# Seven row maxima in a visit: the idle token bank of an MLP's second phase used for one more score matmul

## The chip, the cores and the metric

The kernel runs on one core of a Trainium2 chip. The metric is the device time of one launch in microseconds (us), as the median of several runs. Engines go by the profile's names: PE is TensorE's matmuls, PEld its weight loads, DVE is VectorE, ACT ScalarE, POOL GpSimd and SP the queue that issues most DMAs. PSUM, into which TensorE writes, has 8 banks of 512 fp32 columns on 128 partitions. The kernel holds all of it as one tile, `bank[:, 0..7]`.

## The reference

For 2048 tokens of width 448, with x the common input:

```
g = sigmoid(sum(x * gate_w))
a = mha_block(x)                 # 16 heads of 28: qkv, softmax(q k^T * 28^-0.5), p v, wo
h = gelu(layernorm(x) @ w1 + b1) # 448 -> 1792, tanh form
b = h @ w2 + b2                  # 1792 -> 448
out = g * a + (1 - g) * b
```

The kernel's softmax subtracts the maximum of each query's row of scores. These maxima are the work that the change regroups: 16 heads x 16 query tiles of 128 x 4 pieces of 512 keys, so 1024 score matmuls of [28 x 128] by [28 x 512], each with a maximum over its 512 columns.

## The kernel before, in words

The work runs in three stages: projections of q, k, v; the MLP, during which nearly half of the row maxima are taken; and attention, during which the rest are taken. The core's instructions stand in program order on every engine from the third token chunk of the projections on, and on TensorE throughout.

**The MLP** works on four chunks c of 512 tokens, each in two phases. In the first (`mlp1`, line 564) each of 14 feature tiles f takes 11 matmuls of 512 columns into bank `f % 2`, from which ScalarE takes two gelus. In the second (`mlp2`, line 579) each of four token tiles i takes 14 x 3 = 42 matmuls of 448 columns (lines 585, 586 and 590) which accumulate in bank `i % 2`; ScalarE then copies that bank out (line 596). So in the second phase one of the banks 0 and 1 accumulates, and the other holds the last tile until it is copied and then nothing until the next tile begins.

**Row maxima beside the MLP.** After matmuls of the MLP the kernel calls `filler.run(n)` (line 449), which adds n to a slot counter. `due` (line 442) spreads the maxima evenly over the slots of the whole MLP: `MLP_MAX` = 482 of them over about 248 slots, where a matmul of the second phase counts 0.205 (line 590's call adds that, the call before it twice that). When as many are due as a visit takes (`MG` = 6, or what is left), a **visit** is issued: `RowMax.issue(2, 6)` (line 374) puts six score matmuls (line 402) into banks 2 to 7, between two matmuls of the MLP. The four heads of a group lie in four strips of 32 rows of the array; successive score matmuls go round them (head j in rows 32j to 32j+27). Every 65th place in this order holds instead a transpose of 16 finished columns (`close`, line 366).

**The maxima on VectorE.** `reduce` in `issue` takes the banks in order, two at a time where it can: line 384 reduces two neighbouring banks in one instruction, line 382 one bank. Two are taken together only if the second's place in `mx` lies after the first's, which fails each time the heads wrap from 3 to 0 between them. A score matmul waits for the reduce that read its bank in the visit before; `close` adds `mt` (line 371), and the last of 64 pieces adds `mf` (line 418).

**After the MLP** attention issues single maxima into banks 5 and 6 (`scores`, line 515) until all 1040 places are done. The first five scores of attention are put beside the last token tile (line 594). Bank 7 serves that tile and then the sums of p v.

The lines that set the order of the visits:

```
            if self.max is not None and self.due(n) >= min(MG, self.upto - self.done) > 0:
                self.max.issue(2, min(MG, self.upto - self.done))
...
        due = self.first + (self.upto - self.first) * min(1, self.slot / self.slots) - self.done
```

Of the kernel before, what the change touches and what calls it, by code (L numbers as in the profile page):

```python
# [26 lines left out]
NF = F // P  # L27
# [5 lines left out]
MG = 6  # L33
FS = 4
W1, W2 = 0.233, 0.205
# [6 lines left out]
def kernel(ctx: ExitStack, tc: tile.TileContext, xt, wqk, wv, wo, xk, w1, b1, w2, b2,  # L42
# [300 lines left out]
    class RowMax:  # L343
# [27 lines left out]
            nc.vector.tensor_scalar(mt, ps[:4 * TPC, :P], -1.0, None, op0=OP.mult)  # L371
            self.queue.dma_start(ms[g][:, c * CH:(c + 1) * CH].rearrange("j (i x) -> j i x", x=P), mt.bitcast(F32))

        def issue(self, first, n, rows=None):

            held = []

            def reduce():
                if held:
                    (b0, c0), (b1, c1) = held[0], held[-1]  # L380
                    if b0 == b1:
                        nc.vector.reduce_max(self.mx[:, c0:c0 + 1], bank[:, b0], axis=AX)  # L382
                    else:
                        nc.vector.reduce_max(self.mx[:, c0:c1 + 1:c1 - c0], bank[:, b0:b1 + 1], axis=AX)  # L384
                    held.clear()

            for b in range(first, first + n):
                if self.done >= NG * NC * 65:
                    break
                self.done += 1  # L390
                left = sum(len(x) for x in self.left)
                if self.last is not None and (left <= 56 or self.n == NG * NC):
                    reduce()
                    self.close(bank[:, b])
                    continue
                most = max(range(4), key=lambda j: (len(self.left[j]), -j))
                j = max(rows, key=lambda j: len(self.left[j])) if rows else most
                if not self.left[j]:
                    j = most
                i, k = self.left[j].pop(0)  # L400
                r = slice(32 * j, 32 * j + DH)
                nc.tensor.matmul(bank[:, b], self.qds[self.n][r, i * P:(i + 1) * P],  # L402
                                 khi[self.n // NC][r, k * 512:(k + 1) * 512], start=True, stop=True)
                at = (j * TPC + i) * 4 + k
                if held and held[0][1] > at:
                    reduce()
                held.append((b, at))
                if len(held) == 2:
                    reduce()
                if left == 41 and self.n + 1 < NG * NC:  # L410
                    self.load(self.n + 1)
                g, c = divmod(self.n, NC)
                if c == NC - 1 and g < MLP_G and all(n != k for x in self.left for _, n in x):
                    load_khr(g + 1, k)
                if left == 1:
                    reduce()
                    self.last = mpool.tile([P, 4 * TPC], F32, name="mf")
                    nc.vector.reduce_max(self.last, self.mx.rearrange("p (a k) -> p a k", k=4), axis=AX)
                    if self.n + 1 < NG * NC:
                        self.begin(self.n + 1)  # L420
                    else:
                        self.n += 1
                        self.left = [[]] * 4
            reduce()

    class Filler:
# [19 lines left out]
            left = self.upto - self.done  # L446
            return left if self.slot >= self.slots else min(left, int(due))

        def run(self, n=1):


            if self.max is not None and self.due(n) >= min(MG, self.upto - self.done) > 0:
                self.max.issue(2, min(MG, self.upto - self.done))

    filler = Filler()

# [3 lines left out]
    def load_khr(g, k=None, queue=nc.sync):  # L460

        sl = slice(0, S) if k is None else slice(k * CH, (k + 1) * CH)
        for j in range(4):
            r = D + (4 * g + j) * DH
            queue.dma_start(khr[32 * j:32 * j + DH, sl].bitcast(F32), qk[0, r:r + DH, sl])
# [38 lines left out]
    def load_qm(n):  # L504

        while filler.done < min(65 * NG * NC, 65 * (n + 1) + 9):
            filler.max.issue(5, 1)
        g, c = divmod(n, NC)
        nc.sync.dma_start(qs[n][0][DH:P:32].bitcast(F32), ms[g][:, c * CH:(c + 1) * CH])

# [4 lines left out]
    def scores(units, most, tiles, between=None):  # L515

        def product(p, i):
            u = units[p]  # L520
            n, k, j = u // 4 // NT, u // 4 % NT, u % 4
            g, (qh, ql) = n // NC, qs[n]
            a, b, r = ((khi[g], qh, DH + 1), (klo[g], qh, DH), (khi[g], ql, DH))[i]
            r = slice(32 * j, 32 * j + r)
            nc.tensor.matmul(bank[:, p], a[r, k * P:(k + 1) * P], b[r], start=(i == 0), stop=(i == 2))  # L525

        def exps(at):
            t = tiles(len(at), at[0])
            nc.scalar.activation(t, bank[:, at[0]:at[-1] + 1], AF.Exp, scale=SCALE)  # L529
            for i, p in enumerate(at):  # L530
                probs[units[p]] = t[:, i]

        first, last = list(range(len(units)))[:UA], list(range(len(units)))[UA:]
        if most > 0:
            filler.max.issue(5, 1, [(units[0] + 3) % 4])
        for i in range(3):
            for p in first:
                product(p, i)
        exps(first)
        if between:  # L540
            between()
        for i in range(3):
            for p in last:
                product(p, i)
            if i == 0 and most > 1:
                filler.max.issue(6, 1, [(units[0] + 1) % 4, (units[0] + 2) % 4])
        if last:
            exps(last)
        if most > 2:
            filler.max.issue(5, 1, [(units[0] + 1) % 4, (units[0] + 2) % 4])  # L550


    ml = ExitStack()
# [25 lines left out]
    def mlp2(c, i):  # L579

        sl = slice(i * P, (i + 1) * P)
        last = c * TPC + i == NT - 1
        a = bank[:, 7 if last else i % 2, :D]
        for f in range(NF):
            nc.tensor.matmul(a, hh[f][:, sl], w2h[f], start=(f == 0), stop=False)  # L585
            nc.tensor.matmul(a, hh[f][:, sl], w2l[f], start=False, stop=False)  # L586
            rows = not last and (c * TPC + i < NT - 2 or f < 10) and (c + i > 0 or f > 3)
            if rows:
                filler.run(2 * W2)
            nc.tensor.matmul(a, hl[f][:, sl], w2h[f], start=False, stop=(f == NF - 1))  # L590
            if rows:
                filler.run(W2)
            if last and f == NF // 3:
                scores(list(range(U)), 0, early)
        gb = mh.tile([P, CH], F32, name="h", bufs=2)[:, :D]
        nc.scalar.activation(gb, a, AF.Copy)  # L596
        nc.sync.dma_start(gbs[c * TPC + i], gb)

    with texts:
# [12 lines left out]
        for c in range(NC):  # L612
# [23 lines left out]
            if c == NC - 1:  # L636
                m0.close()
                aq = ctx.enter_context(tc.tile_pool(name="aq", bufs=1, side="right", reuse_waits="tile"))

                first = {3: aq.tile([P, S], F32, name="klo", bufs=2), 2: aq.tile([P, NT, P], F32, name="vg", bufs=2)}  # L640

                def early(n, p):
                    t = first[n] if n == 3 else first[n].rearrange("p a b -> p (a b)")
                    return t[:, :n * CH].rearrange("p (n c) -> p n c", c=CH)

                nc.scalar.activation(gate, zall, AF.Exp, scale=-1.0)
                load_khi(0)
                load_klo(0)
                load_q(0)
                load_v(0)  # L650
                load_qm(0)
            else:
                ln_load(c + 1)
                ln_fetch(c + 1, 0)
                ln_fetch(c + 1, 1)
            for i in range(TPC):
                mlp2(c, i)
                if c == NC - 1 and i == 0:
                    nc.vector.tensor_scalar_add(gate, gate, 1.0)
                    nc.vector.reciprocal(gate, gate)  # L660
                    nc.vector.tensor_scalar(ngate, gate, -1.0, 1.0, op0=OP.mult, op1=OP.add)
                if c + 1 < NC and i < 3:
                    ln_apply(c + 1, i)
                    if i < 2:
                        ln_fetch(c + 1, i + 2)
                    else:
                        ln_apply(c + 1, 3)
# [125 lines left out]
    with tc.manual_schedule(engines=ENGINES):  # L793
# [3 lines left out]
        at = -1  # L797
# [3 lines left out]
        while u < 4 * steps:  # L801
# [3 lines left out]
            units = list(range(u, min(u + (UL if late else U), 4 * steps)))  # L805
            while at < units[-1] // 4:
                at += 1
                n, k = divmod(at, NT)
# [43 lines left out]
            if u:  # L852
                scores(units, min(3, filler.due()), pt, (lambda: values(ready - 1)) if late else None)
# [3 lines left out]
            if ended:  # L857
                n = summed // NT - 1
# [62 lines left out]
```

## Time and profile before

| | |
|---|---|
| Median of 3 runs | 1119.53 us (1119.23 to 1121.82) |
| The profiled execution | 1119.32 us, of which the span of its instructions is 1117.5 us |
| PE busy | 1105.8 us (99%) |
| DVE, ACT, POOL busy | 738.9 us (66%), 634.4 us (57%), 333.4 us (30%) |
| Granted TensorE clock | 1.0 of full speed in all slices |
| The four second phases of the MLP | begin at 158, 247, 337 and 427 us of the span |

A timeline row gives the start in us from the beginning of the span, the length in us, the engine, the line of the kernel, the operation, the tile written <- the tiles read, shapes, and "xN" where neighbouring instructions of one kind are merged; in brackets stands how long the engine was idle before it, and what ended that. A row of a merged group has one start and the length until the last of the group ends. A matmul's length is modelled and holds its way through the array, so matmuls that follow each other overlap: their starts are what one reads. A row of the groups by line gives a count, the summed busy time, the mean of one in ns, and the idle time before them.

### The profile page before, as it was taken

How to read it: one execution, taken by the hardware profiler on the slowest of the kernel's cores; microseconds unless marked ns; L12 is line 12 of the kernel's file. 1: busy time of each engine (PE TensorE's matmuls, PEld its weight loads, DVE VectorE, ACT ScalarE, POOL GpSimd, SP SyncE). 2: the span in 40 equal slices, each digit the busy share in tenths (PEclk: the TensorE clock that was granted, in tenths of full speed). 3: DMA queues.
4: the chain of work that ended last, by engine and by line, in shares of the span. 5: the costliest groups of instructions: out<-in, count | busy, mean ns of one | idle time of the engine just before them, and what ended most of it. 6: DMA issues, size and time to landing. Idle time of an engine off the chain costs nothing.

```text
span 1117.5 us, 19782 instructions
## 1 busy us (share of the span) xinstructions
PE 1105.8 (99%) x8136; PEld 672.7 (60%) x8136; DVE 738.9 (66%) x1029; ACT 634.4 (57%) x662; POOL 333.4 (30%) x354
## 2 busy tenths in 40 slices
PE   7999999999999999999999999999999999999998
PEld 5888777777777777744444444444444444454546
DVE  3534398988889889576766766676667767746103
ACT  5324551230241132288787877887877878847572
POOL 4006665343334331013113221320223024342350
PEclk9999999999999999999999999999999999999999
DMA  8988541011120113163100220012021003002111
GB/s 263 302 273 309 170 135 58 9 47 36 50 55 32 30 43 96 38 157 89 28 18 19 61 69 22 22 28 52 26 60 36 18 20 94 12 26 70 55 32 58
DMA packets 53079, 84.35 MB, mean 75 GB/s; under 512 B 8516, under 2 KB 28500, under 8 KB 52076
## 3 DMA queue, kind: packets, MB, share of 16 engines
q1 hardware_dynamic: 48732, 76.27, 22.7%
q0 software_dynamic: 4256, 6.81, 2.5%
q8 instruction: 64, 1.05, 0.4%
q14 instruction: 27, 0.22, 0.1%
HBM read 56.40 MB, written 26.49 MB: 74 GB/s over the span
## 4 chain that ended last, share of the span: by engine, by line
PE 96%; DMA 2%; DVE 1%; ACT 1%; POOL 0%; SPq 0%; issue 0%
PE bank L788 22%; PE bank L525 20%; PE bank L402 16%; PE bank L572 13%; PE bank L207 5%; PE bank L590 5%; PE bank L585 4%; PE bank L586 4%; PE bank L223 3%; PE bank L693 1%; PE bank L694 1%; PE bank L695 1%; DMA raw<-in_xt 1%; DMA raw<-in_wqk 1%; DMA raw<-in_wv 0%; DMA s<-in_w 0%
## 5 line engine op out<-in xcount | busy, mean ns | idle before, releaser
L529 ACT ACTIVATE pt<-bank 128x1536 f32<-128x1536 f32 (+1 forms) x387 | 461.9, 1244 | 141.0 <-PE bank L525 140.8
L382 DVE TENSOR_REDUCE mx<-bank 128x1 f32<-128x512 f32 x618 | 409.6, 687 | 173.1 <-PE bank L402 159.1
L788 PE MATMUL bank<-pt,vg 128*32 128x512 f32 x1950 | 261.6, 602 | 0.0
L384 DVE TENSOR_REDUCE mx<-bank 128x2 f32<-128x1024 f32 x203 | 238.9, 1219 | 29.2 <-PE bank L402 28.8
L402 PE MATMUL bank<-khi,qd 28*128 28x512 f32 x512 | 241.7, 479 | 0.1
L402 PEld LDWEIGHTS bank<-khi,qd 28*128 28x128 f32 x512 | 92.3, 181 | 148.1 <-DVE mx L382 106.9
L525 PE MATMUL bank<-qh,klo 28*128 28x512 f32 x1024 | 174.7, 393 | 0.0
L525 PE MATMUL bank<-qh,khi 29*128 29x512 f32 x768 | 157.2, 480 | 0.0
L572 PE MATMUL bank<-y,w1f 128*128 128x512 f32 x616 | 152.4, 398 | 1.1 <-ACT h L576 1.1
L572 PEld LDWEIGHTS bank<-y,w1f 128*128 128x128 f32 x616 | 112.5, 188 | 34.8 <-issue 10.9
L525 PE MATMUL bank<-ql,khi 28*128 28x512 f32 x768 | 129.6, 390 | 0.0
L577 POOL TENSOR_TENSOR hl<-h,hh 128x512 fp32r<-128x512 f32 x56 | 73.7, 1317 | 117.5 <-ACT h L576 77.3
L788 PEld LDWEIGHTS bank<-pt,vg 128*32 128x32 f32 x1950 | 44.6, 108 | 77.2 <-issue 76.7
L525 PEld LDWEIGHTS bank<-qh,klo 28*128 28x128 f32 x1024 | 87.6, 185 | 4.0
L575 ACT ACTIVATE hh<-bank,b1s 128x512 fp32r<-128x512 f32 x56 | 38.5, 687 | 90.3 <-PE bank L572 90.3
L709 POOL DMA_DIRECT2D lt<-ob x15 | 10.9, 725 | 250.9 <-DVE ob L708 250.9
L596 ACT ACTIVATE h<-bank 128x448 f32<-128x448 f32 x16 | 8.7, 545 | 134.5 <-PE bank L590 100.2
L590 PE MATMUL bank<-w2h,hl 128*128 128x448 f32 x224 | 85.0, 379 | 0.0
L525 PEld LDWEIGHTS bank<-qh,khi 29*128 29x128 f32 x768 | 60.8, 181 | 39.6 <-ACT pt L529 26.7
L585 PE MATMUL bank<-w2h,hh 128*128 128x448 f32 x224 | 83.3, 372 | 0.0
L586 PE MATMUL bank<-w2l,hh 128*128 128x448 f32 x224 | 81.9, 365 | 0.0
L402 PE MATMUL bank<-khr,qd 28*128 28x512 f32 x512 | 80.1, 467 | 0.2 <-DVE mx L384 0.2
(122 smaller groups left out, 1294.6 us busy)
## 6 DMA issues: line engine op xcount, KB each, us to landing
qk<-hl SPq DMA_DIRECT2D x28, 512.0 KB
raw<-in_xt SPq DMA_DIRECT2D x16, 256.0 KB
vs<-vt SPq DMA_DIRECT2D x16, 256.0 KB
s<-in_xt SPq DMA_DIRECT2D x16, 256.0 KB
rc<-rls POOLq DMA_DIRECT2D x60, 64.0 KB, 2.2
bxr<-in_xk SPq DMA_DIRECT2D x8, 448.0 KB
gbs<-h SPq DMA_DIRECT2D x16, 224.0 KB
klo<-qk SPq DMA_DIRECT2D x16, 224.0 KB
```

The costliest lines, as they stand in the source:

```text
L207: nc.tensor.matmul(ps, a, b, start=(i == 0), stop=(i == len(ops) - 1))
L382: nc.vector.reduce_max(self.mx[:, c0:c0 + 1], bank[:, b0], axis=AX)
L384: nc.vector.reduce_max(self.mx[:, c0:c1 + 1:c1 - c0], bank[:, b0:b1 + 1], axis=AX)
L402: nc.tensor.matmul(bank[:, b], self.qds[self.n][r, i * P:(i + 1) * P], khi[self.n // NC][r, k * 512:(k + 1) * 512], start=True, stop=True)
L525: nc.tensor.matmul(bank[:, p], a[r, k * P:(k + 1) * P], b[r], start=(i == 0), stop=(i == 2))
L529: nc.scalar.activation(t, bank[:, at[0]:at[-1] + 1], AF.Exp, scale=SCALE)
L572: nc.tensor.matmul(ps, a, b, start=(i == 0), stop=(i == len(ops) - 1))
L577: nc.gpsimd.tensor_sub(hl[f], h, hh[f].bitcast(F32))
L585: nc.tensor.matmul(a, hh[f][:, sl], w2h[f], start=(f == 0), stop=False)
L586: nc.tensor.matmul(a, hh[f][:, sl], w2l[f], start=False, stop=False)
L590: nc.tensor.matmul(a, hl[f][:, sl], w2h[f], start=False, stop=(f == NF - 1))
L788: nc.tensor.matmul(pv[32 * j:32 * j + 32, :], vg[n // NC][:, k, 32 * j:32 * j + 32], probs.pop(4 * step + j), start=(k == 0), stop=(k == N ...
```

## The change

`issue` takes a list of banks in place of a first bank and a count. `run` takes a list `more` of banks that are put ahead of the banks 2 to 7, and a visit is issued only when as many maxima are due as it has banks. `mlp2` passes the other token bank, `(i + 1) % 2`, for f from 2 to 10. A pair in `reduce` must now also lie in neighbouring banks. All other calls of `issue` pass the banks that they used before.

```
-        def issue(self, first, n, rows=None):
+        def issue(self, banks, rows=None):
...
-            for b in range(first, first + n):
+            for b in banks:
...
-                if held and held[0][1] > at:
+                if held and (held[0][1] > at or held[0][0] + 1 != b):
                     reduce()
...
-        def run(self, n=1):
+        def run(self, n=1, more=()):
...
-            if self.max is not None and self.due(n) >= min(MG, self.upto - self.done) > 0:
-                self.max.issue(2, min(MG, self.upto - self.done))
+            if self.max is not None:
+                banks = [*more, *range(2, 2 + MG)][:self.upto - self.done]
+                if self.due(n) >= len(banks) > 0:
+                    self.max.issue(banks)
...
             rows = not last and (c * TPC + i < NT - 2 or f < 10) and (c + i > 0 or f > 3)
+
+            more = [(i + 1) % 2] if 2 <= f <= NF - 4 else []
             if rows:
-                filler.run(2 * W2)
+                filler.run(2 * W2, more)
             nc.tensor.matmul(a, hl[f][:, sl], w2h[f], start=False, stop=(f == NF - 1))
             if rows:
-                filler.run(W2)
+                filler.run(W2, more)
```

More of the change, by code (lines that the diff above doesn't have):

```diff
@@ L506, in load_qm @@
         while filler.done < min(65 * NG * NC, 65 * (n + 1) + 9):
-            filler.max.issue(5, 1)
+            filler.max.issue([5])
         g, c = divmod(n, NC)
@@ L534, in scores @@
         if most > 0:
-            filler.max.issue(5, 1, [(units[0] + 3) % 4])
+            filler.max.issue([5], [(units[0] + 3) % 4])
         for i in range(3):
@@ L545, in scores @@
             if i == 0 and most > 1:
-                filler.max.issue(6, 1, [(units[0] + 1) % 4, (units[0] + 2) % 4])
+                filler.max.issue([6], [(units[0] + 1) % 4, (units[0] + 2) % 4])
         if last:
@@ L549, in scores @@
         if most > 2:
-            filler.max.issue(5, 1, [(units[0] + 1) % 4, (units[0] + 2) % 4])
+            filler.max.issue([5], [(units[0] + 1) % 4, (units[0] + 2) % 4])
     ml = ExitStack()
```

## The prediction

> **What bounds the kernel now.** I read the page's busy times and chain first, then the groups by line, then the timeline inside a second phase of the MLP.
>
> ```profile
> span 1117.5 us, 19782 instructions
> PE 1105.8 (99%) x8136; PEld 672.7 (60%) x8136; DVE 738.9 (66%) x1029; ACT 634.4 (57%) x662; POOL 333.4 (30%) x354
> PE 96%; DMA 2%; DVE 1%; ACT 1%; POOL 0%; SPq 0%; issue 0%
> ```
>
> TensorE carries 96% of the chain that ended last, so a visit costs what it takes out of TensorE's stream. One visit of six, chunk 2, token tile 0:
>
> ```profile
> 340.09 0.36 PE L590 MATMUL bank<-w2h,hl 128*128 128x448 f32 x1
> 340.38 0.73 PE L402 MATMUL bank<-khr,qd 28*128 28x512 f32 x6
> 340.92 3.49 DVE L384 TENSOR_REDUCE mx<-bank 128x2 f32<-128x1024 f32 x3 [0.41 <-PE bank L402]
> 341.04 0.47 PE L585 MATMUL bank<-w2h,hh 128*128 128x448 f32 x1
> 341.35 0.36 PE L586 MATMUL bank<-w2l,hh 128*128 128x448 f32 x1
> ...
> 343.97 0.36 PE L590 MATMUL bank<-w2h,hl 128*128 128x448 f32 x1
> 344.27 0.74 PE L402 MATMUL bank<-khr,qd 28*128 28x512 f32 x6
> ```
>
> From 341.35 to 343.97 thirteen matmuls start, 0.202 us apart. From 340.09 to 341.35 are two such steps, 0.40, and 0.86 that the visit costs. So the next visit, 15 steps later, starts 15 x 0.202 + 0.86 = 3.89 after this one (3.89 in the rows). VectorE begins 0.54 after the visit's first matmul and needs 3.49: it is done 4.03 after it, later than the next visit starts, and yet nothing waits. Why that is, and how near it is to waiting, a second view tells:
>
> ```profile
> 340.72 0.39 PE L402 MATMUL bank<-khr,qd 28*128 28x512 f32 x2
> ```
>
> The last two of the six start 0.33 after the first four, and they write banks 6 and 7. So bank 7 is wanted 3.89 + 0.33 = 4.22 after the visit's start, and is free at 4.03: 0.19 to spare. VectorE is 66% busy over the span, but in this stage it is nearly full.
>
> **What the change does to the visits.** I took the order of TensorE's instructions from the built programs. All matmuls of the MLP and of attention stand in the same order, attention's maxima too; 482 maxima are done beside the MLP as before. In the second phases 40 visits of six and one of two become 21 of seven, 15 of six and one of five (size@matmuls of the tile already issued less one; tiles divided by bars, chunks by lines; two tiles have none or a lone one):
>
> ```
> 7@23 6@38 | 7@14 7@32 | 6@5 7@22 6@37 | 7@13 7@31
> 7@13 7@31 | 6@4 7@22 6@37 | 7@11 7@29 | 6@2 7@20 6@35
> 7@16 6@34 | 6@5 7@22 6@37 | 7@13 7@31 | 6@4 7@22 6@37
> 6@1 7@19 6@34 | 7@10 7@26 6@41 | 7@17 5@29 |
> ```
>
> Sevens come 18 steps apart. But near a tile's ends, where the other bank isn't offered, six are enough again: a six follows a seven after only 15 steps, sometimes fewer.
>
> **The seventh matmul on TensorE.** How a visit's length goes with its size:
>
> ```profile
> 359.65 0.36 PE L590 MATMUL bank<-w2h,hl 128*128 128x448 f32 x1
> 359.94 0.50 PE L402 MATMUL bank<-khr,qd 28*128 28x512 f32 x2
> 360.37 0.28 PE L368 MATMUL bank<-ident,mf 128*16 128x128 f32 x1
> 360.58 0.50 PE L402 MATMUL bank<-khr,qd 28*128 28x512 f32 x3
> 361.00 0.19 PEld L585 LDWEIGHTS bank<-w2h,hh 128*128 128x128 f32 x1 [0.24 <-issue]
> ...
> 190.01 0.36 PE L586 MATMUL bank<-w2l,hh 128*128 128x448 f32 x1
> 190.21 0.27 PE L368 MATMUL bank<-ident,mf 128*16 128x128 f32 x1
> 190.41 0.73 PE L402 MATMUL bank<-khr,qd 28*128 28x512 f32 x5
> 191.07 0.47 PE L590 MATMUL bank<-w2h,hl 128*128 128x448 f32 x1
> ```
>
> Two and three take 0.50, five and six 0.73: matmuls on different strips run at once, four in a round, and the second round starts 0.33 later. Seven are four and three, two rounds as before. I cost the seventh at nothing; the other end is a sixth of a visit, 0.14, and below nothing it cannot be. By the Trainium skill ("TensorE: Matmul & The Clock Gate", Part 1) warm matmuls of 512 columns that follow each other start 215.7 ns apart; were the seventh such a step, 21 of them would add an estimated 4.5 us, less what they take out of the waits below. The rows of three in 0.50 speak against it.
>
> **Visits saved.** 37 in place of 41. The visit of two was a dear one:
>
> ```profile
> 457.49 0.37 PE L590 MATMUL bank<-w2h,hl 128*128 128x448 f32 x1
> 457.78 0.50 PE L402 MATMUL bank<-khr,qd 28*128 28x512 f32 x1
> 458.47 0.49 PE L402 MATMUL bank<-khr,qd 28*128 28x512 f32 x1 [0.18 <-DVE mx L384]
> 459.20 0.36 PE L586 MATMUL bank<-w2l,hh 128*128 128x448 f32 x1
> ```
>
> 1.71 less two steps is 1.31. So 40 x 0.86 + 1.31 = 35.7 becomes 37 x 0.86 = 31.8: **-3.9**. Transposes cost extra where they break a round. In the rows above, the next plain matmul comes 1.06 after the last one where the transpose is first (190.01 to 191.07) and 1.35 where it is third (359.65 to 361.00); a plain visit has 0.95. So 0.11 or 0.40. Before, the four in these phases stand third, first, fifth and first; after, third, first, first and once sixth behind a second round (there 0.63 + 0.42 + 0.21 + 0.42 less 0.96, so 0.72). **+0.3**.
>
> **The new waits.** VectorE gets one bank more. A visit with its heads out of step shows the single reduce, and what a late one costs:
>
> ```profile
> 380.37 0.77 PE L402 MATMUL bank<-khr,qd 28*128 28x512 f32 x6
> 380.89 0.69 DVE L382 TENSOR_REDUCE mx<-bank 128x1 f32<-128x512 f32 x1 [0.31 <-PE bank L402]
> 381.50 2.35 DVE L384 TENSOR_REDUCE mx<-bank 128x2 f32<-128x1024 f32 x2
> 383.76 0.68 DVE L382 TENSOR_REDUCE mx<-bank 128x1 f32<-128x512 f32 x1
> 383.98 1.01 PE L402 MATMUL bank<-khr,qd 28*128 28x512 f32 x6
> 384.50 0.18 PEld L402 LDWEIGHTS bank<-khr,qd 28*128 28x128 f32 x1 [0.22 <-DVE mx L382]
> 384.93 0.50 PE L572 MATMUL bank<-y,w1f 128*128 128x512 f32 x1
> ```
>
> A single reduce steps 0.61 and ends after 0.69, a pair steps 1.13. Bank 7's reduce ends at 384.44; TensorE, which wanted it at 383.98 + 0.33 = 384.31, gets it at 384.50, and the next plain matmul starts 0.95 after the visit's first, not 0.66. A wait of 0.19 cost 0.29: the weight load that lay beside the other matmuls is bare, 0.1.
>
> Seven banks are three pairs and a single, or two pairs and three singles: 0.54 + 3.39 + 0.69 = 4.62 or 0.54 + 2.26 + 1.22 + 0.69 = 4.71, where the spare bank's reduce goes first. Released 0.06 later, the second round can go at 4.68 or more. A seven 18 steps later wants it at 18 x 0.202 + 0.86 + 0.33 = 4.83: 0.15 to spare. A six 15 steps later wants it at 4.22: it waits 0.46, and with the bare load costs **0.55**.
>
> Such sixes, from the list: 0.0@38, 0.2@5, 0.2@37, 1.1@4, 1.1@37, 1.3@35, 2.1@37, 2.3@4, 2.3@37 and 3.0@34, ten. (At 1.3@2 and 3.1@41 the seven before holds a transpose, so only six reduces.) The first visit of chunk 1 comes 10 + 4 steps after a seven, 0.66; a six follows a six after 13 steps at 2.1@5, 0.3 to 0.4. Sum 5.5 + 0.66 + 0.35 = **+6.5**. The queue behind a waiting matmul is all of TensorE's; VectorE isn't delayed by it, since it has the six's first pair by then, so one wait does not breed the next.
>
> Four such waits stand in the trace of before, the one above and these:
>
> ```profile
> 186.64 0.18 PEld L402 LDWEIGHTS bank<-khr,qd 28*128 28x128 f32 x2 [0.25 <-DVE mx L384]
> ...
> 400.44 0.18 PEld L402 LDWEIGHTS bank<-khr,qd 28*128 28x128 f32 x1 [0.22 <-DVE mx L382]
> ...
> 444.50 0.18 PEld L402 LDWEIGHTS bank<-khr,qd 28*128 28x128 f32 x2 [0.30 <-DVE mx L384]
> ```
>
> At about 0.25 each they make 1.0; I take half as gone, since places and pairings shift: **-0.5**.
>
> **What I cost at nothing.** The spare bank must be copied out before its first score matmul:
>
> ```profile
> 189.60 0.36 PE L590 MATMUL bank<-w2h,hl 128*128 128x448 f32 x1
> 190.05 0.55 ACT L596 ACTIVATE h<-bank 128x448 f32<-128x448 f32 x1 [9.35 <-issue]
> ```
>
> The copy is over 1.0 after the tile's last matmul starts. The earliest visit that uses the bank comes 10 steps into a tile, 2.0 us: hidden. The next tile's first matmul needs that bank reduced: the latest such visit is at 32, nine steps or 2.5 us ahead, and its reduce, first in the queue, ends 1.8 after the visit starts. Were it behind two more reduces, it would cost 0.5, once. The stores of `ms` and loads of `qd` on SP move with their visits, beside transfers that nothing waits for here.
>
> **Sum.** -3.9 + 0.3 + 6.5 - 0.5 = +2.4 us. Against the profiled execution, 1119.3, that is 1121.7; the median of the runs lies 0.2 above it, so **1121.8**.
>
> **Rivals.** *The waits don't come* (TensorE's next round is later, or VectorE earlier, than rows tell): -3.9 + 0.3 - 1.0, so 1114.9. For it: before, sixes lie 0.19 clear. Against: at 384.50 TensorE went 0.06 after the reduce. 0.06.
>
> *VectorE becomes the bound of the phase*, the other side. If a seven's reduces end later by d (start after the handoff, or reading banks 1 and 2 as one pair), each of the twelve waits grows by d, and beyond d = 0.15 the six visits 16 to 18 steps after a seven wait too, at d - 0.15 + 0.1. At d = 0.3: 3.6 + 1.5, so 1127; from d = 0.1 on the loss passes 0.3%. For it: 0.15 is little. Against: rows of each reduce. The page "TensorEngine Tiling (Array Packing)" of the Trainium skill, under "PSUM Bottleneck", warns that tiling speeds up TensorE and not the emptying of PSUM, which may then bound; by it the seven fits no better than its reduces. The rows agree for the sixes behind a seven and not for sevens behind sevens. 0.22.
>
> *The seventh costs 0.14*: 21 x 0.14 = 2.9, but a later next visit waits less, twelve times 0.14: net +1.3, 1123.1. 0.08.
>
> **How the numbers follow.** The forecast has 0.64; its own range is 1120 to 1123.3, with twelve waits between 0.4 and 0.65. A measurement of this kernel tells about 0.3%, 3.4 us, from no change, so "slower" begins at 1122.9. Slower: 0.14 of the forecast's, 0.17 of the bound's, 0.04 of the seventh's, 0.35 in all. Faster: most of the first rival's, 0.05. The same: 0.60. The range leaves out the first rival and the far part of the second: 1119.0 to 1125.5.
>
> **What would show it.** Right: sevens whose next plain matmul starts 0.96 after the last one, as after sixes; the row of a weight load of line 402 released by DVE, some 0.4 long, ahead of sixes at the listed places; VectorE's idle time between visits gone there. Wrong: sevens longer than 0.75 of matmul rows; waits at sevens; a wait ahead of line 587, or of ScalarE's copy. Attention, from 472 on, should have the same length.

## The result and the profile after

The changed kernel takes 1120.66 us (median of 22 runs, 1119.96 to 1122.29), the kernel before 1118.85 us (22 runs, 1117.94 to 1122.19): a ratio of 1.0015, 95% interval 1.0009 to 1.002. That is 1.8 us more, less than the 0.3% that the prediction took for "the same", but clear of zero.

The page of the changed kernel, its span, busy times and chain:

```profile
span 1118.4 us, 19804 instructions
PE 1105.3 (99%) x8136; PEld 671.5 (60%) x8136; DVE 737.4 (66%) x1039; ACT 634.1 (57%) x662; POOL 333.4 (30%) x354
PE 92%; DVE 4%; DMA 2%; ACT 1%; POOL 0%; issue 0%; SPq 0%
```

The busy shares haven't moved. The chain has: VectorE's part went from 1% to 4%. A busy time averaged over 1118 us cannot show a dozen waits of half a microsecond; the chain can, since it follows just those steps at which the end was decided. It doesn't price them: at each wait it follows VectorE's reduces back, and counts their whole time, so 3% of the span stand here for 1.8 us. VectorE takes 10 instructions more, as fewer banks are reduced in pairs.

Where the time went: from the first matmul of the MLP's ninth feature tile to the MLP's last matmul it is 331.2 us before and 333.1 after, 1.9 more; from there to the end 646.0 and 645.7. (The spans differ by 0.9 only, as chunk 0's first phase took 0.86 less up to that tile in the profiled execution after: the matmul behind the first visit waited 0.32 for ScalarE's second gelu, where it had waited 1.10, since a transfer that ScalarE needed first had come earlier. All this stands before any of the moved visits.)

Here is a seven and the six behind it, chunk 0, token tile 0, in the timeline of the changed kernel (lines 587, 588 and 594 are the old 585, 586 and 590):

```profile
161.91 0.37 PE L594 MATMUL bank<-w2h,hl 128*128 128x448 f32 x1
162.20 0.73 PE L402 MATMUL bank<-khr,qd 28*128 28x512 f32 x7
162.77 3.49 DVE L384 TENSOR_REDUCE mx<-bank 128x2 f32<-128x1024 f32 x3 [0.70 <-PE bank L402]
162.87 0.47 PE L587 MATMUL bank<-w2h,hh 128*128 128x448 f32 x1
...
165.81 0.37 PE L594 MATMUL bank<-w2h,hl 128*128 128x448 f32 x1
166.11 1.29 PE L402 MATMUL bank<-khr,qd 28*128 28x512 f32 x6
166.17 0.68 DVE L382 TENSOR_REDUCE mx<-bank 128x1 f32<-128x512 f32 x1
166.77 1.22 DVE L384 TENSOR_REDUCE mx<-bank 128x2 f32<-128x1024 f32 x1
166.91 0.18 PEld L402 LDWEIGHTS bank<-khr,qd 28*128 28x128 f32 x1 [0.41 <-DVE mx L382]
167.33 0.47 PE L587 MATMUL bank<-w2h,hh 128*128 128x448 f32 x1
```

Seven score matmuls end 0.73 after they begin, as six did, and the next plain matmul starts 0.67 after the visit (162.87). Three pairs later VectorE reduces bank 7 alone, from 166.17 to 166.85. The six has begun at 166.11 and wanted bank 7 at 166.44. It gets it at 166.91, 0.06 behind the reduce. The next plain matmul starts at 167.33, 1.22 after the visit began where 0.66 is usual: 0.56 lost.

The waits by engine, in the stretch from 157 us to the MLP's end, of the changed kernel (who waited <- for whom: us in total, times, longest):

```profile
PEld bank L402 <- DVE mx L384: 8.8, 23, 0.8
PEld bank L402 <- DVE mx L382: 4.5, 12, 0.4
PE bank L402 <- DVE mx L384: 1.3, 4, 0.5
```

and of the kernel before, the same stretch:

```profile
PEld bank L402 <- DVE mx L384: 7.6, 22, 0.5
PEld bank L402 <- DVE mx L382: 2.4, 8, 0.4
PE bank L402 <- DVE mx L384: 0.2, 1, 0.2
```

Of the 35 waits of `PEld` after, 22 are the 0.3 to 0.4 us that a weight load stands idle ahead of any visit, whichever engine is named last; before, 25 of 30 are. The others lie inside a visit and are the ones that count: 13 after, 5.7 us in all, at the twelve sixes that the prediction lists (one has two), and 5 before, 1.5 us. `PE`, not `PEld`, waits where the array had run dry as well: at four of those sixes after, and once before, in the visit of two.

### The profile page after: what moved, and what is told of

It is laid out like the page before. It is cut to its first block, busy times and chain, and to the rows that moved or that the text cites. A ratio compares the mean times of both kernels' runs of the same rounds, so it can differ in the third digit from the quotient of the medians.

```text
span 1118.4 us, 19804 instructions
## 1 busy us (share of the span) xinstructions
PE 1105.3 (99%) x8136; PEld 671.5 (60%) x8136; DVE 737.4 (66%) x1039; ACT 634.1 (57%) x662; POOL 333.4 (30%) x354
## 4 chain that ended last, share of the span: by engine, by line
PE 92%; DVE 4%; DMA 2%; ACT 1%; POOL 0%; issue 0%; SPq 0%
PE bank L792 22%; PE bank L527 20%; PE bank L402 15%; PE bank L574 13%; PE bank L207 5%; PE bank L587 3%; PE bank L594 3%; PE bank L223 3%; PE bank L588 3%; DVE mx L384 3%; PE bank L697 1%; DVE mx L382 1%; PE bank L698 1%; PE bank L699 1%; DMA raw<-in_wqk 1%; DMA raw<-in_xt 0%
## 5 line engine op out<-in xcount | busy, mean ns | idle before, releaser
L382 DVE TENSOR_REDUCE mx<-bank 128x1 f32<-128x512 f32 x638 | 422.9, 687 | 182.0 <-PE bank L402 168.0
L384 DVE TENSOR_REDUCE mx<-bank 128x2 f32<-128x1024 f32 x193 | 226.7, 1218 | 22.0 <-PE bank L402 22.0
```

## Experiments

Two theories. *Theory*: the seventh matmul is free on TensorE, four visits are saved, and what is lost are sixes that find bank 7 unreduced behind a seven. *Rival*: something about the sevens themselves is dear: the matmul, the copy of the spare bank, or VectorE's work as such. All differences below are against the kernel before, run on the same chip.

**VectorE's work halved in the sevens.**

```
+            cols = slice(0, CH // 2) if len(banks) == MG + 1 else slice(0, CH)
...
-                        nc.vector.reduce_max(self.mx[:, c0:c0 + 1], bank[:, b0], axis=AX)
+                        nc.vector.reduce_max(self.mx[:, c0:c0 + 1], bank[:, b0, cols], axis=AX)
```

(and the pair's line likewise.)

> The changed kernel, but a visit of seven banks reduces only columns 0 to 255 of each bank (the maxima over columns 256 to 511 of those banks are left out). TensorE's stream is as in the changed kernel. Theory (the loss is sixes that wait for VectorE behind a seven): about twelve waits of 0.4 to 0.7 us go, so 6 us less than the changed kernel, 4 us less than the kernel before. Rival (a seven is dear on TensorE itself, or the copy of the spare bank is waited for): the waits were not the cost, the time stays within 1.5 us of the changed kernel, above the kernel before.

1114.58 against 1118.94, ratio 0.9961 (0.9949 to 0.9973): 4.4 us less than before. The changed kernel took 1.8 more, so this is some 6.2 less than it. The same two visits in its timeline:

```profile
162.43 0.73 PE L403 MATMUL bank<-khr,qd 28*128 28x512 f32 x7
163.00 1.89 DVE L385 TENSOR_REDUCE mx<-bank 128x2 f32<-128x512 f32 x3 [0.69 <-PE bank L403]
164.80 0.41 DVE L383 TENSOR_REDUCE mx<-bank 128x1 f32<-128x256 f32 x1
166.33 0.73 PE L403 MATMUL bank<-khr,qd 28*128 28x512 f32 x6
167.00 0.47 PE L588 MATMUL bank<-w2h,hh 128*128 128x448 f32 x1
```

VectorE is done 1.1 us before the six, which runs its 0.73. All twelve waits but one are gone: the six that comes 13 matmuls behind a six (chunk 2, token tile 1) still loses 0.4, since visits of six reduce as much as before. TensorE's order is that of the changed kernel, so all of the loss and 4 us of hidden gain lay in waiting for VectorE. The rival falls in all but VectorE's work as such, which the next two runs leave as it is.

**Sixes held back until seven are due.**

```
-                if self.due(n) >= len(banks) > 0:
+                if self.due(n) >= min(max(least, len(banks)), self.upto - self.done) > 0:
...
-                filler.run(2 * W2, more)
+                filler.run(2 * W2, more, MG + 1)
```

> The changed kernel, but in the second phase a visit of six banks, too, waits until seven maxima are due, so sixes come 17 or 18 matmuls behind a seven in place of 15. Theory: most waits of sixes shrink from 0.5 to 0.6 us to 0.4 and less, as many visits are left; 4 us less than the changed kernel, 2 us less than the kernel before. Rival (sevens themselves are dear): there are 22 of them in place of 21, so the time stays that of the changed kernel.

1116.35 against 1118.94, ratio 0.9977 (0.9968 to 0.9985): 2.6 us less than before, on the expectation's side and a little beyond it. No reduce is shorter here and none is left out; only the distance from a seven to a six has grown, from 15 to mostly 18 matmuls. What is left shows above all in the three sixes that come after 16, which lose 0.3 to 0.4 each. One of them (chunk 1, token tile 1) follows a seven that begins with a single; four reduces behind that are merged to 4.76:

```profile
255.39 0.76 PE L402 MATMUL bank<-khr,qd 28*128 28x512 f32 x7
255.92 0.69 DVE L382 TENSOR_REDUCE mx<-bank 128x1 f32<-128x512 f32 x1 [0.32 <-PE bank L402]
256.52 4.76 DVE L384 TENSOR_REDUCE mx<-bank 128x2 f32<-128x1024 f32 x4
259.52 1.04 PE L402 MATMUL bank<-khr,qd 28*128 28x512 f32 x6
260.05 0.18 PEld L402 LDWEIGHTS bank<-khr,qd 28*128 28x128 f32 x2 [0.35 <-DVE mx L384]
260.49 0.47 PE L587 MATMUL bank<-w2h,hh 128*128 128x448 f32 x1
```

Banks 6 and 7 were the last pair, wanted at 259.52 + 0.33 = 259.85 and had at 260.05: 0.2 late, and 0.3 lost. (The fourth of the merged reduces is the six's first: VectorE went on without a gap, so one wait does not cause the next.) A seven 17 matmuls behind a seven (chunk 0, token tile 2) lost 0.19: what sevens have to spare at 18 is less than one step of 0.2.

**The spare bank last.**

```
-                banks = [*more, *range(2, 2 + MG)][:self.upto - self.done]
+                banks = [*range(2, 2 + MG), *more][:self.upto - self.done]
...
-            more = [(i + 1) % 2] if 2 <= f <= NF - 4 else []
+            more = [(i + 1) % 2] if 2 <= f <= 7 else []
```

> The changed kernel with the spare bank as the last of the seven in place of the first, and offered for f from 2 to 7 only (15 sevens), so that the next tile doesn't wait for its reduce. Theory: VectorE is done with bank 7 as early as after a visit of six, the following six finds it free, and only the spare bank's reduce ends late, which nobody wants by then: waits of sixes behind sevens gone, 5 us less than the changed kernel, 3 us less than the kernel before. Rival (VectorE has too little time in all, whatever the order): as much VectorE work per seven, so at least half of the loss against the kernel before stays, and the time is above the kernel before.

1116.99 against 1118.94, ratio 0.9981 (0.9972 to 0.999): 2.0 us less, in the theory's direction, at two thirds of its size. The mechanism is in the rows of its first seven and six:

```profile
162.68 0.73 PE L402 MATMUL bank<-khr,qd 28*128 28x512 f32 x7
163.22 3.49 DVE L384 TENSOR_REDUCE mx<-bank 128x2 f32<-128x1024 f32 x3 [0.67 <-PE bank L402]
166.59 0.73 PE L402 MATMUL bank<-khr,qd 28*128 28x512 f32 x6
166.63 0.68 DVE L382 TENSOR_REDUCE mx<-bank 128x1 f32<-128x512 f32 x1
167.24 0.47 PE L587 MATMUL bank<-w2h,hh 128*128 128x448 f32 x1
```

VectorE does as much in as long a time: its last reduce ends at 167.31, 4.63 after the seven began, where it was 4.65 in the changed kernel. But this one is the spare bank's, which the six doesn't use. The six takes its 0.73 and the next plain matmul comes 0.65 after it began. So it isn't VectorE's work that cost, but which bank was read last. Of the missing microsecond, 0.4 are four sixes of the second phases behind which the plain matmul came about 0.1 late. Transposes make up the rest: the visits moved, and all seven of the MLP now stand second to fifth in their visit and cost 0.4 each, 2.8 in all, where before two stood first (0.11 each) and one last (0.02), 1.9 in all.

**A seventh matmul alone**, in the kernel before:

```
                 self.max.issue(2, min(MG, self.upto - self.done))
+                if more is not None:
+                    ...
+                    nc.tensor.matmul(bank[:, more], m.qds[m.n][r, 0:P], khi[m.n // NC][r, 0:512], start=True, stop=True)
+                    nc.vector.tensor_copy(scrap, bank[:, more, 0:1])
```

> The kernel before with 27 of its visits in the second phases followed by a seventh score matmul into the spare token bank, whose result nobody uses (one column of it is copied away by VectorE). No visit is saved or moved, and VectorE gets no seventh reduce. Theory (a seventh runs beside the fifth and sixth): the time of the kernel before within 1 us. Rival (a seventh costs a sixth of a visit, 0.14 us, or a matmul's step of 0.2 us): 4 to 5 us more than the kernel before.

1131.15 against 1118.94, ratio 1.0103 (1.0087 to 1.0119): 12 us more, where the theory said 1 and the rival 4 to 5. Neither had it. The extra matmuls are not the cause: in the first such visit the next plain matmul comes 0.66 after the visit began, as without one. The wait is elsewhere, above all at the first matmul of the token tiles (line 592 there):

```profile
PEld bank L592 <- DVE scrap L460: 6.0, 5, 1.6
PE bank L592 <- DVE scrap L460: 4.1, 5, 1.2
```

The copy of one column stood behind the visit's reduces in VectorE's queue, and the next token tile needs that bank. Five token tiles begin 0.5 to 1.4 us late, 5.0 in all, and a chunk's first feature tile, which needs bank 0, 1.3. Another 1.8 went at the visit of two, whose extra matmul waited for the copy before it; most of the rest is told under the last heading. With the copy moved ahead of the reduces, and the matmul to the front of the visit, on the strip ahead of the visit's first:

```
+                if more is not None:
+                    ...
+                    nc.tensor.matmul(bank[:, more], m.qds[m.n][r, 0:P], khi[m.n // NC][r, 0:512], start=True, stop=True)
+                    nc.vector.tensor_copy(scrap, bank[:, more, 0:1])
                 self.max.issue(2, min(MG, self.upto - self.done))
```

> The kernel before with 27 of its visits in the second phases preceded by one more score matmul into the spare token bank, whose result nobody uses (VectorE copies one column of it, now ahead of the visit's reduces, where it was behind them in the run with the matmul at the visit's end). TensorE's matmuls and strips are those of a visit of seven. Theory (a seventh costs nothing on TensorE; the 12 us of that run were next tiles that waited for the copy): within 1 us of the kernel before. Rival (the extra matmul itself costs 0.14 us or more): 4 us more than the kernel before, or above.

1119.53 against 1118.87, ratio 1.0007 (0.9998 to 1.0015): at most 1.7 us for 27 matmuls and 27 copies, where a seventh at 0.14 would be 3.8. Its timeline:

```profile
162.39 0.49 PE L458 MATMUL bank<-khr,qd 28*128 28x512 f32 x1
162.39 0.73 PE L403 MATMUL bank<-khr,qd 28*128 28x512 f32 x6
162.92 0.16 DVE L459 COPY scrap<-bank 128x1 f32<-128x1 f32 x1 [0.56 <-PE bank L403]
162.99 3.48 DVE L385 TENSOR_REDUCE mx<-bank 128x2 f32<-128x1024 f32 x3
163.05 0.48 PE L598 MATMUL bank<-w2h,hl 128*128 128x448 f32 x1
```

The seven go in two rounds, and the next plain matmul comes 0.66 after the visit began. The seventh is free within that bound.

**The spare bank last, over the whole range of f**, so `2 <= f <= NF - 4` is kept:

```
-                banks = [*more, *range(2, 2 + MG)][:self.upto - self.done]
+                banks = [*range(2, 2 + MG), *more][:self.upto - self.done]
```

> The changed kernel with the spare bank as the last of the seven, as in the run with the spare bank last, but offered for f up to 10 as in the changed kernel. Theory: sixes behind sevens no longer wait, but five visits late in a tile leave the spare bank's reduce some 4.7 us behind the visit's start, and the next tile's first matmul, which comes after 2.5 to 3 us, waits 0.9 to 2 us for it: 5 us more than the kernel before. Rival (the order of the banks alone matters, the range of f doesn't): 2 us less than the kernel before, as with the spare bank last and f up to 7.

1127.76 against 1118.87, ratio 1.0084 (1.0066 to 1.0101): 8.9 us more, worse than the theory's 5 and far from the rival's. The waits stand where they were expected. One of the long ones, chunk 2, token tile 3:

```profile
374.22 0.54 ACT L600 ACTIVATE h<-bank 128x448 f32<-128x448 f32 x1 [9.22 <-PE bank L594]
375.19 0.68 DVE L382 TENSOR_REDUCE mx<-bank 128x1 f32<-128x512 f32 x1
375.92 0.47 PE L587 MATMUL bank<-w2h,hh 128*128 128x448 f32 x1 [1.74 <-DVE mx L382]
```

The tile's first matmul starts 2.11 after the matmul before it, and the spare bank's reduce had ended 0.05 earlier. Four token tiles and a chunk's first feature tile begin late like this, 1.0 to 2.1 us behind the usual step of 0.2, 8.8 in all; less the 3.9 that the saved visits give, that is the theory's 5. So the changed kernel needed the spare bank first for its range of f, and it is this choice that put bank 7 last. The rest of the 8.9 is told under the last heading.

## Why the prediction was right

It said 1121.8 with "the same" the likeliest and slower the likelier side; 1120.66 is in its own narrow range. The mechanism was right too, not the number alone. Of the 1.1 us between them, 0.7 is the start: the sum set out from three runs of the kernel before, 1119.53, and 22 runs give 1118.85. (From 1119.53 and +2.4 the sum is 1121.9, not 1121.8.) The change itself was put at +2.4 and measured at +1.8. By its steps:

- **The seventh at nothing**: right. The 18 sevens without a transpose go 1.26 to 1.29 us from the last matmul before to the second after, as sixes without a wait did (1.25 to 1.31), and the extra matmul alone cost 0.7 in 27, at most 1.7.
- **Visits saved, -3.9**: right in kind. With VectorE's work halved, so that only one six still waits, the kernel is 4.4 faster than before; -3.9, +0.3 for the transposes, -1.0 for all the old waits and +0.4 for that six make -4.2.
- **Transposes, +0.3**: right. First in a visit they cost 0.11, third 0.40, and sixth behind a second round 0.69 (0.72 was forecast).
- **Twelve new waits, +6.5**: right in place, number and size. All twelve that the list named are there and no thirteenth. They cost 0.56, 0.60, 0.39, 0.71, 0.51, 0.59, 0.61, 0.38, 0.79, 0.56, 0.53 and 0.53, 6.8 in all. The 0.79 is a visit in which `mf` stood ahead of bank 7's reduce.
- **Old waits, -0.5**: the mis-sized term. All four are gone, about -1.0. With it the sum is -3.9 + 0.3 + 6.8 - 1.0 = +2.2, and the MLP took 1.9 more.
- **At nothing**: ScalarE's copy and the next tile's first matmul: right, with no row of line 587 waiting for VectorE. That the second of them is a real term as soon as the spare bank's reduce ends later, the last experiment shows.

Of the rivals, VectorE as the bound of the whole phase did not come: no seven behind a seven waits. What the Trainium skill says under "PSUM Bottleneck" ("TensorEngine Tiling (Array Packing)"), that tiling speeds up TensorE and not the emptying of PSUM, did decide the sign, but at twelve places and not on the average. By "TensorE: Matmul & The Clock Gate" (Part 1) of the Trainium skill, a warm matmul of 512 columns starts 215.7 ns after the last. In this kernel's trace those of the MLP's first phase start some 228 ns apart; scores on other strips don't wait that long, as the rows of seven in 0.73 show.

## What to carry to other kernels

When a producer's burst grows, ask not only whether the consumer keeps up on average: write down when each buffer is wanted and when it is free, for the shortest distance between two bursts. The order in which the consumer frees the buffers is then a free choice: here the loss of 1.8 us hung on which bank was freed last, and either more distance (2.6 us faster than before) or another order with a narrower range of f (2.0 faster) turned it into a gain. Both are faster than either kernel; between the two the runs don't decide, as their intervals overlap. Another order has its own price: over the whole range of f it made the next tile wait, and cost 8.9.

## What the runs showed of the hardware

A wait of TensorE of about 2 us may cost more than itself. In the run with the spare bank last over the whole range, the granted clock (the column after POOL's) falls behind the wait at 375.9:

```profile
375.00:376.00 1.00, 0.08 (x1) 0.08 (x1) 0.87 (x2) 0.28 (x1) 0.65 (x1) 1.00 0.38 142
376.00:377.00 1.00, 1.00 (x5) 0.78 (x5) 0.00 (x0) 0.00 (x0) 1.00 (x2) 1.00 0.54 178
377.00:378.00 1.00, 1.00 (x7) 0.40 (x6) 0.14 (x1) 0.00 (x0) 0.92 (x2) 0.63 0.62 137
378.00:379.00 1.00, 1.00 (x4) 0.78 (x3) 1.00 (x1) 0.00 (x0) 1.00 (x1) 0.50 0.01 2
379.00:380.00 1.00, 1.00 (x4) 0.87 (x4) 1.00 (x3) 0.63 (x1) 0.26 (x2) 0.50 0.00 0
380.00:381.00 1.00, 1.00 (x5) 0.90 (x4) 1.00 (x2) 0.00 (x0) 1.00 (x1) 0.66 0.00 0
381.00:384.00 3.00, 3.00 (x19) 2.19 (x19) 0.72 (x2) 0.00 (x0) 0.23 (x1) 1.00 0.00 0
```

It is 1.00 for another 1.3 us, then half for about 3.4 us: some 1.7 us lost after the wait had ended. Three other waits as long in the same execution, ending at 179.6, 203.3 and 261.5, brought no such drop. That the wait caused this one is read from its place alone, and what sets it apart from the three was not tested. Over the six executions of this kernel the mean granted clock goes from 1.0 (1124.72 us) to 0.994 (1131.65 us), and 0.006 of 1123 us is 6.7 of the 6.9 us between them. The execution at 1.0 is 5.9 us above the kernel before and the median 8.9: the 3 us between are, by the clock, this. In the run with the copy behind the reduces the clock was at 0.5 from 467.3 to 474.1 as well, from within the wait of the visit of two on; at half the clock these 6.8 us lose 3.4. "TensorE: Matmul & The Clock Gate" in the Trainium skill (Part 1) has the clock halved after an idle window of about 3.4 us; here it halved after the array had stood idle for 1.74 us, with work before and behind.
